# P V of a cached-attention decode kernel: from V standing to P standing in four column tiles

## Chip, cores, metric

One core of a Trainium2 chip. The metric is the time of one execution of the whole program in microseconds (us), as the device measures it; the median of three runs is compared. The profile is one further execution, taken by the hardware profiler.

## What is computed

One decode step for 8 sequences: attention over the last 2048 positions of a cache, then an MLP block. Cut to what matters here:

```
q = layernorm(x) @ wq                         # 8 x 32 heads x 128
k, v = last 2048 positions of the caches      # 8 sequences x 8 kv heads x 2048 x 128
p = softmax(q k^T / sqrt(128))                # 4 query heads share a kv head
o = p v                                       # the step that is changed
h = x + o @ wo
out = h + B(layernorm(h))                     # B: w3, gelu, w4 (its token shift is zero for S = 1)
```

k and v are 33.5 MB each in bfloat16; with wq, wo, w3 and w4 the kernel reads 79.18 MB.

## The kernel before

**Units.** The work on the caches is cut into 16 units: unit n is sequence b = n // 2 and half t = n % 2 of its kv heads (J = 4 heads). A unit of K or V is one 2 MB load onto 128 partitions, partition 32 j + r holding 64 consecutive positions of head j. `knat` and `vnat` have four buffers each. All loads stand on SP's queue in one fixed order. A load of K waits until PE has transposed the unit that was in its buffer (`e_T`), a load of V until PE has done P V on its buffer (`e_PV`). wo comes in parts (two of 1 MB at n = 5 and 9, four of 512 KB at the end), and w3 and w4 go into freed buffers of K at the end: w3 (`sem_w3`), then w4 in three groups `sem_w4a`, `sem_w4b`, `sem_w4c`.

**One iteration of the loop over n.** PE turns the four parts of a unit of K (`turn_K`, 8 transposes in 32 bits each, L296); ACT evicts the lower half of each part (L283), DVE the upper (L284). After the third part comes the first `pe_QK`, after the fourth the second (L311: 8 matmuls of 512 columns, 32 columns of q standing, in four column tiles). P V runs three units behind K (four for the last two), one block w = 0..3 at a time (`pe_PV`), where `pvs(k)` stands.

**Softmax.** After the odd unit of a sequence: maximum (`softmax_1`, L321), two small 32-bit matmuls with DVE steps between them (`softmax_2`, `softmax_3`, L325 to L339), Exp on ACT (L342). In the next even iteration DVE spreads P into a sparse `Pz` in four parts (L355, each behind one of K's evictions), PE multiplies row sums with ones (`softmax_5`, L372), DVE takes the reciprocal (L375, L381), PE transposes P (`softmax_4`, L364) and the result `pS` is evicted by the same helper as K. The row sums, the maximum's row and column, and `turn_o`'s result share one PSUM bank, `sm`; `sm_read` holds the last DVE operation that read it, and every matmul into it waits for that.

**P V, and what follows it.** Of a block, 16 chunks of V (128 positions x 128) stand one after the other while 16 columns of P move (L397); 64 matmuls of a unit add up in 16 columns of `oT_ps`. `scale` (DVE, L407) reads them out, multiplies with the reciprocal row sums and writes `oK`; the next unit's P V waits for it. `turn_o` (4 matmuls, L417) brings the heads into the order that wo wants, and a DVE copy (L422) puts them into `o2`.

**The tail.** After the loop DVE spreads the last P (four times L355 in a row), and PE does units 12 to 15 of P V, softmax of the last sequence and wo: groups 0 to 3 after the first block of unit 15, groups 4 and 5, 6 and 7 at the end, each pair with its own load (L458). Then hsum (L559), the statistics (L562, L583), w3 (L579), gelu (L597), w4 (L607), a transpose and the store.

Operations are recorded per engine in the order in which they are written in the code, each with its waits, and emitted at the end: every engine runs its list in that order. `turn_os(to)` records `turn_o` for all units below `to` that have not had it.

Of the kernel before, what the change touches and what calls it, by code (L numbers as in the profile page):

```python
# [6 lines left out]
dt = mybir.dt  # L7
ACT = mybir.ActivationFunctionType
ALU = mybir.AluOpType
AX = mybir.AxisListType  # L10
# [3 lines left out]
H = 32  # L14
DH = 128
G = 8
R = H // G
# [11 lines left out]
NU = 2  # L29
J = G // NU  # L30
U = 4
# [5 lines left out]
NV = 4  # L37
NKT = 4
LVD = 3
WO_AT = (5, 9)  # L40
WO_G = (0, 2)
WO_L = 4
QW = 12 + R + 28
SPR = 4


# [30 lines left out]
def bass_sequential_preLN__sliding_block_cached__mixer_s_mlp__decode_kernel(  # L77
# [19 lines left out]
    NUN = NB * NU  # L97
# [4 lines left out]
    with es:  # L102
        sb = lambda shape, dtype, name: es.enter_context(nc.sbuf_tensor(name, shape, dtype))
# [4 lines left out]
        vnat = sb([128, NV, UL], dt.bfloat16, "vnat")  # L108
# [6 lines left out]
        ident_f = sb([128, 128], dt.float32, "ident_f")  # L115
# [36 lines left out]
        mK = sb([128, R], dt.float32, "mK")  # L152
        rLk = sb([128, 2, H, R], dt.float32, "rLk")
        oK = sb([128, 2, J, R, R], dt.bfloat16, "oK")
        o2 = sb([128, G, R, B], dt.bfloat16, "o2")

        NH = KC * B
        tail = Pz[:, 0, :].bitcast(dt.float32)
        at = [0]
# [30 lines left out]
        def dma(eng, dst, src, sem, *waits):  # L190
            def f(e):
# [25 lines left out]
        e_sel = DV.op(lambda e: e.tensor_reduce(sel_f[:, :].rearrange("p (j h) -> p j h", j=J),  # L217
                                                ident_f[:, :].rearrange("p (j u h) -> p j h u", j=J, u=U),
                                                AX.X, ALU.add), e_idf)
        e_mE = DV.op(lambda e: e.tensor_reduce(mE[:, :], ident_f[:, :].rearrange("p (e k) -> p e k", k=R),  # L220
                                               AX.X, ALU.max))
        e_mK = DV.op(lambda e: e.tensor_reduce(mK[:, :], ident_f[:, :].rearrange("p (e k) -> p k e", k=R),
# [41 lines left out]

        def fill_q(b):
            for c in range(2):
                at = 12 + 16 * c
# [34 lines left out]
        def pe_QK(m):  # L302
            n, v = divmod(m, 2)
            b, t = divmod(n, NU)
            lo = 12 - 8 * v - 4 * t
            kT = kT_sb[:, (2 * m) % NKT:(2 * m) % NKT + 2, :].rearrange("p u (c j r k) -> p j k (u c) r", c=8, j=J, k=2)

            def f(e):
                for k in range(2):
                    for j in range(J):  # L310
                        ins = e.matmul(S_ps[b % 2][32 * j:32 * (j + 1), :].rearrange("p (c r) -> p c r", c=16),  # L311
                                       qz[:, b % 2, J * t + j, k, lo:lo + 32], kT[:, j, k],
                                       start=(t == 0 and v == 0 and k == 0), stop=(t == NU - 1 and v == 1 and k == 1),
                                       tile_position=(0, 32 * j), skip_group_check=True)
                return ins
            e_QK[m] = PE.op(f, *e_ev[2 * m], *e_ev[2 * m + 1], e_qw[b], e_qs, e_exp.get(b - 2))
# [7 lines left out]
        def softmax_2(b):  # L324
            e_mT[b] = PE.op(lambda e: e.matmul(sm[0:1, MROW], mcol[:, :], ident_f[:, :], start=True, stop=True),  # L325
                            e_max[b], sm_read[0], e_idf)
            e = DV.op(lambda e: e.tensor_reduce(Mrow[:, :].rearrange("o (j h) -> o j h", j=J),  # L327
                                                sm[0:1, MROW].rearrange("o (j u h) -> o j h u", j=J, u=U),
                                                AX.X, ALU.max), e_mT[b])
            sm_read[0] = e  # L330
            m_bc = bass.AP(tensor=Mrow[:, :].tensor, offset=0, ap=[[H, 1], [8, J], [0, U], [1, 8]])
            e_neg[b] = DV.op(lambda e: e.tensor_scalar(negrow[:, :].rearrange("o (j u h) -> o j u h", j=J, u=U), m_bc,  # L332
                                                       -1.0, None, ALU.mult), e, e_negps.get(b - 1))

        def softmax_3(b):
# [47 lines left out]
        def V(n, w):  # L383
            if n == NUN - 1:
                return sem_vl[w], 16
            return sem_v[n % NV], 16 * (n // NV + 1)

        def pe_PV(i):
            n, w = divmod(i, U)
            b, t = divmod(n, NU)  # L390
            dst = oT_ps[:, 0:16]

            def f(e):
                for c in range(16):
                    o = (8 * (w % 2) + c // 2) * 128 + 16 * (2 * (2 * (c % 2) + w // 2) + t)
                    mvg = pS[:, b % 2, o:o + 16]
                    ins = e.matmul(dst, vnat[:, n % NV, (16 * w + c) * DH:(16 * w + c + 1) * DH], mvg,  # L397
                                   start=(w == 0 and c == 0), stop=(w == U - 1 and c == 15),
                                   skip_group_check=True)
                return ins  # L400
            e_PV[i] = PE.op(f, V(n, w), *e_pS[b], e_sc.get(n - 1))

        def scale(n):
            b, t = divmod(n, NU)
            src = oT_ps[:, 0:16]
            s_bc = bass.AP(tensor=src.tensor, offset=src.offset, ap=[src.ap[0], [1, 16], [0, R]])
            e_sc[n] = DV.op(lambda e: e.tensor_tensor(oK[:, n % 2].rearrange("p g r k -> p (g r) k"), s_bc,  # L407
                                                      rLk[:, b % 2, 16 * t:16 * t + 16, :], ALU.mult),
                            e_rL[b], e_PV[U * n + U - 1], e_scale.get(n - 2))

        def turn_o(n):
            b, t = divmod(n, NU)
# [49 lines left out]
            e_wo.append(PE.op(f, e_exp[NB - 2], X, *waits))  # L462

        def emit_PV(i):
            if i % U == 1 and i > U:
                turn_os(i // U)
                if i // U == NUN - 1:
                    pe_wo((0, 1, 2, 3), e_scale[NUN - NU], (sem_wo, 16 * len(WO_AT)))
            pe_PV(i)
            if i % U == U - 1:  # L470
                scale(i // U)

        pv = [0]
        turned = [0]

        def turn_os(to):
            while turned[0] < to:
                turn_o(turned[0])
                turned[0] += 1
# [6 lines left out]
        for n in range(NUN):  # L486
# [17 lines left out]
                fill_q(b)  # L504
            turn_K(i)
            spread(0)
            turn_os(pv[0] // U)
            turn_K(i + 1)
            spread(1)
            turn_K(i + 2)  # L510
            spread(2)
            pe_QK(2 * n)
            if t == 0 and b >= 1:
                softmax_5(b - 1)
            turn_K(i + 3)
# [17 lines left out]
        softmax_5(NB - 1)  # L533
        softmax_4(NB - 1)
        emit_PVs(NBLK)
        turn_o(NUN - 1)
        for a in range(2):
            for g in (WO_L + 2 * a, WO_L + 2 * a + 1):
                load_wo(g, sem_wl[a], 1)
# [43 lines left out]
        e = PE.op(lambda e: e.matmul(st2, ones_v[:, :], vsum[:, :], start=True, stop=True), e_vs, e_sc[NUN - 1])  # L583
# [72 lines left out]
```

## Time and profile before

| | us |
|---|---|
| runs | 197.91, 197.44, 197.72; median 197.72 |
| profiled execution | 197.34 |
| its span, first to last instruction | 196.0 |
| PE busy, matmuls | 153.8 (78% of the span) |
| PE weight loads (beside the matmuls) | 125.9 (64%) |
| DVE / ACT / POOL busy | 98.2 / 85.9 / 7.0 |
| mean granted clock of TensorE | 0.872 |
| read from HBM | 79.18 MB, 404 GB/s over the span |

The largest groups of PE are K's transposes (L296, 512 matmuls, 76.1), P V (L397, 1024, 33.2) and q K (L311, 256, 20.0). PE's matmuls are pipelined and their ends are modelled, so busy time of PE is no measure of what it could do. An idle is listed with the operation that ended it; "issue" means that the engine waited for nothing that the profile shows.

### The profile page before, as it was taken

How to read it: one execution, taken by the hardware profiler on the slowest of the kernel's cores; microseconds unless marked ns; L12 is line 12 of the kernel's file. 1: busy time of each engine (PE TensorE's matmuls, PEld its weight loads, DVE VectorE, ACT ScalarE, POOL GpSimd, SP SyncE). 2: the span in 40 equal slices, each digit the busy share in tenths (PEclk: the TensorE clock that was granted, in tenths of full speed). 3: DMA queues.
4: the chain of work that ended last, by engine and by line, in shares of the span. 5: the costliest groups of instructions: out<-in, count | busy, mean ns of one | idle time of the engine just before them, and what ended most of it. 6: DMA issues, size and time to landing. Idle time of an engine off the chain costs nothing.

```text
span 196.0 us, 5301 instructions
## 1 busy us (share of the span) xinstructions
PE 153.8 (78%) x2415; PEld 125.9 (64%) x2415; DVE 98.2 (50%) x223; ACT 85.9 (44%) x100; POOL 7.0 (4%) x28
## 2 busy tenths in 40 slices
PE   0038985978989898989885789898989897888464
PEld 0037852765869577868773668586958585777453
DVE  5302444865484566548553384549455765620130
ACT  6001565764456374735471355535635482230030
POOL 4001001001000100010001000100000000000000
PEclk9999999999699999997999579969997999555555
DMA  6999999999999999999999999999999999999970
GB/s 229 461 408 431 425 431 431 421 428 425 423 420 422 431 425 428 423 425 428 419 427 421 431 428 425 428 425 428 425 428 421 423 421 428 407 405 407 406 285 24
DMA packets 7542, 79.52 MB, mean 406 GB/s; under 512 B 856, under 2 KB 864, under 8 KB 3424
## 3 DMA queue, kind: packets, MB, share of 16 engines
q1 hardware_dynamic: 7504, 79.18, 96.1%
q8 instruction: 19, 0.31, 0.6%
q14 instruction: 3, 0.02, 0.0%
q10 hardware_dynamic: 16, 0.01, 0.0%
HBM read 79.18 MB, written 0.01 MB: 404 GB/s over the span
## 4 chain that ended last, share of the span: by engine, by line
DMA 51%; PE 31%; DVE 10%; SPq 5%; issue 2%
DMA knat<-in_A_k_cache_dram 42%; PE kT_ps L296 21%; DMA knat<-in_B_w_dram 9%; SPq L192 5%; PE S_ps L311 5%; DVE kT_sb L284 5%; DVE Pz L355 2%; PE kT_ps L364 2%; DVE mcol L321 1%; PE oT_ps L397 1%; PE sm L325 1%; PE sm L336 1%; DVE Mrow L327 1%; PE S_ps L607 1%; DVE negrow L332 0%
## 5 line engine op out<-in xcount | busy, mean ns | idle before, releaser
L283 ACT ACTIVATE kT_sb<-kT_ps 128x1024 bf16<-128x1024 bf16 x64 | 63.8, 1024 | 47.2 <-PE kT_ps L296 46.5
L296 PE MATMUL kT_ps<-perm_k,knat 128*128 128x128 f32 x512 | 76.1, 306 | 3.4 <-DMA knat<-in_A_k_cache_dram 3.2
L296 PEld LDWEIGHTS kT_ps<-perm_k,knat 128*128 128x128 f32 x512 | 65.7, 159 | 9.1 <-issue 4.3
L284 DVE TENSOR_SCALAR kT_sb<-kT_ps 128x512 int32<-128x512 int32 x64 | 44.2, 690 | 35.0 <-PE kT_ps L296 34.8
L397 PEld LDWEIGHTS oT_ps<-pS,vnat 128*128 128x128 bf16 x1024 | 30.5, 98 | 6.4 <-issue 6.1
L397 PE MATMUL oT_ps<-pS,vnat 128*128 128x16 bf16 x1024 | 33.2, 171 | 1.3 <-DVE oK L407 1.3
L311 PE MATMUL S_ps<-kT_sb,qz 128*32 128x512 bf16 x256 | 20.0, 386 | 11.0 <-DVE kT_sb L284 10.6
L355 DVE TENSOR_TENSOR Pz<-P_sb,mJ 128x512 bf16<-128x512 bf16 x32 | 21.6, 684 | 0.0
L342 ACT ACTIVATE P_sb<-S_ps,negcol 128x512 bf16<-128x512 f32 x8 | 5.5, 688 | 24.9 <-DVE negcol L339 24.9
L283 ACT ACTIVATE pS<-kT_ps 128x1024 bf16<-128x1024 bf16 x8 | 8.2, 1024 | 15.8 <-PE kT_ps L364 15.8
L311 PEld LDWEIGHTS S_ps<-kT_sb,qz 128*32 128x32 bf16 x256 | 4.7, 94 | 15.8 <-ACT kT_sb L283 14.8
L284 DVE TENSOR_SCALAR pS<-kT_ps 128x512 int32<-128x512 int32 x8 | 5.5, 692 | 9.4 <-PE kT_ps L364 9.4
L364 PEld LDWEIGHTS kT_ps<-perm_p,Pz 128*128 128x128 bf16 x128 | 8.1, 105 | 3.0 <-issue 3.0
L250 PE MATMUL S_ps<-xlnT,wbig 128*128 128x8 bf16 x128 | 3.6, 168 | 7.7 <-DMA wbig<-in_A_wq_dram 7.7
L364 PE MATMUL kT_ps<-perm_p,Pz 128*128 128x128 bf16 x128 | 9.4, 231 | 0.0
L407 DVE TENSOR_TENSOR oK<-oT_ps,rLk 128x64 bf16<-128x64 f32 x16 | 3.6, 224 | 11.1 <-PE oT_ps L397 11.1
L268 POOL COPY qz<-q_sb 64x64 bf16<-64x64 bf16 x16 | 4.6, 290 | 119.7 <-PE S_ps L311 103.5
L321 DVE TENSOR_REDUCE mcol<-S_ps 128x1 f32<-128x512 f32 x8 | 5.5, 692 | 6.5 <-PE S_ps L311 6.5
L250 PEld LDWEIGHTS S_ps<-xlnT,wbig 128*128 128x128 bf16 x128 | 3.5, 104 | 7.7 <-issue 7.7
L584 ACT ACTIVATE Pz<-oT_ps,eps 128x8 f32<-128x8 f32 x1 | 0.3, 268 | 15.0 <-PE oT_ps L583 15.0
L458 PE MATMUL S_ps<-o,wbig 128*128 128x8 bf16 x128 | 4.0, 168 | 2.3 <-issue 2.0
L255 DVE TENSOR_SCALAR kT_sb<-S_ps 128x256 bf16<-128x256 f32 x1 | 0.4, 425 | 10.0 <-PE S_ps L250 10.0
(83 smaller groups left out, 73.3 us busy)
## 6 DMA issues: line engine op xcount, KB each, us to landing
knat<-in_A_k_cache_dram SPq DMA_DIRECT2D x16, 2048.0 KB, 28.9
vnat<-in_A_v_cache_dram SPq DMA_DIRECT2D x15, 2048.0 KB, 30.8
wbig<-in_A_wq_dram SPq DMA_DIRECT2D x1, 4096.0 KB, 12.2
wbig<-in_A_wo_dram SPq DMA_DIRECT2D x2, 1024.0 KB, 30.8
vnat<-in_A_v_cache_dram SPq DMA_DIRECT2D x4, 512.0 KB, 9.4
wbig<-in_A_wo_dram SPq DMA_DIRECT2D x4, 512.0 KB, 11.8
knat<-in_B_w_dram SPq DMA_DIRECT2D x4, 448.0 KB, 13.0
knat<-in_B_w_dram SPq DMA_DIRECT2D x3, 512.0 KB, 16.6
```

Of the source, the lines that this page charges most:

```text
L192: e.dma_start(dst, src).then_inc(sem, 16)
L250: ins = e.matmul(S_ps[0][:, h * B:(h + 1) * B], wq_v[:, kc, h * DH:(h + 1) * DH], xlnT[:, kc * B:(kc + 1) * B], start=(kc == 0), stop=(kc ...
L268: e_qw[b] = PO.op(lambda e, c=c, at=at: e.tensor_copy(qz[64 * c:64 * (c + 1), b % 2, :, :, at:at + R], q_sb[64 * c:64 * (c + 1), :, :, b]. ...
L283: e_lo.append(AC.op(lambda e: e.activation(dst[:, 0:1024], ps[:, 0:1024], ACT.Copy), e_Tlo[k], *free))
L284: e_hi.append(DV.op(lambda e: e.tensor_single_scalar(dst[:, 1024:2048].bitcast(dt.int32), ps[:, 1024:2048].bitcast(dt.int32), 0, ALU.bitwi ...
L296: ins = e.matmul(ps[:, c * 128:(c + 1) * 128], src[:, c * 128:(c + 1) * 128], perm_k[:, :], is_transpose=True)
L311: ins = e.matmul(S_ps[b % 2][32 * j:32 * (j + 1), :].rearrange("p (c r) -> p c r", c=16), qz[:, b % 2, J * t + j, k, lo:lo + 32], kT[:, j, k],
L321: e_max[b] = DV.op(lambda e: e.tensor_reduce(mcol[:, :], S_ps[b % 2][:, :], AX.X, ALU.max), e_QK[4 * b + 3], e_mT.get(b - 1))
L342: e_exp[b] = AC.op(lambda e: e.activation(P_sb[:, :], S_ps[s][:, :], ACT.Exp, bias=negcol[:, s:s + 1], scale=1.0, accum_out=lcol[:, s:s + 1]),
L355: e_Pz[b, part] = DV.op(lambda e: e.tensor_tensor(Pz[:, 0, J * w * part:J * w * (part + 1)].rearrange("p (x j) -> p x j", j=J), p_bc, m_bc ...
L364: ins = e.matmul(ps[:, c * 128:(c + 1) * 128], Pz[:, 0, c * 128:(c + 1) * 128], perm_p[:, :], is_transpose=True)
L397: ins = e.matmul(dst, vnat[:, n % NV, (16 * w + c) * DH:(16 * w + c + 1) * DH], mvg, start=(w == 0 and c == 0), stop=(w == U - 1 and c == 15),
```

## The change

In a block of P V, 32 columns of P now stand and two chunks of V (256 columns) move. A block is 8 matmuls; matmul c goes to column tile c % 4, whose 32 output partitions and 256 columns of `oT_ps` it adds to. Units alternate between the two halves of the bank. Of each tile's 32 x 256 result only 16 rows of each chunk are wanted. ACT evicts 128 x 256 in 32 bits into `oE` (`evict_o`), and `fold` multiplies each of its two 128 x 128 halves, standing, with 16 columns of a 0/1 matrix `selo`, which picks the wanted rows, adds the four tiles and leaves o transposed in 16 columns of `sm`. `scale`'s multiplication reads these. For this the halves that q is placed in (`QW`, `at`, `lo`) and the row sums' and maxima's order (`sel_f`, `Mrow`, `negrow`) are rearranged.

The order changes too. A unit's fold follows the first part of K in the next iteration, where `turn_o` stood; `turn_o` follows the first `pe_QK`, directly before `softmax_5`. In the tail the fold of a unit stands after the next unit's block 0 and `turn_o` after block 1. wo's groups 0 and 1 come after block 1 of unit 15, groups 2 and 3 after block 3. The next unit's P V waits for `evict_o`.

```diff
-QW = 12 + R + 28
+QW = 24 + 32
+VP = 1
+MO = 32 * VP
+NO = 256 * VP
+TO = 128 // MO
...
+        oE = sb([128, 512], dt.float32, "oE")
+        selo = sb([128, MO], dt.float32, "selo")
...
+        e_selo = DV.op(lambda e: e.tensor_reduce(selo[:, :], ident_f[:, :].rearrange("p (a x) -> p x a", a=TO),
+                                                 AX.X, ALU.add))
...
-            lo = 12 - 8 * v - 4 * t
+            lo = 24 - 16 * t - 8 * v
...
         def pe_PV(i):
             n, w = divmod(i, U)
             b, t = divmod(n, NU)
-            dst = oT_ps[:, 0:16]
 
             def f(e):
-                for c in range(16):
-                    o = (8 * (w % 2) + c // 2) * 128 + 16 * (2 * (2 * (c % 2) + w // 2) + t)
-                    mvg = pS[:, b % 2, o:o + 16]
-                    ins = e.matmul(dst, vnat[:, n % NV, (16 * w + c) * DH:(16 * w + c + 1) * DH], mvg,
-                                   start=(w == 0 and c == 0), stop=(w == U - 1 and c == 15),
-                                   skip_group_check=True)
+                for c in range(8):
+                    o = (8 * (w % 2) + c) * 128 + 16 * (4 * t + 2 * (w // 2))
+                    q = c % TO
+                    ins = e.matmul(oT_ps[MO * q:MO * (q + 1), NO * (n % 2):NO * (n % 2 + 1)], pS[:, b % 2, o:o + MO],
+                                   vnat[:, n % NV, (16 * w + 2 * c) * DH:(16 * w + 2 * c + 2) * DH],
+                                   start=(w == 0 and c < TO), stop=(w == U - 1 and c >= 8 - TO),
+                                   tile_position=(0, MO * q), skip_group_check=True)
                 return ins
-            e_PV[i] = PE.op(f, V(n, w), *e_pS[b], e_sc.get(n - 1))
+            e_PV[i] = PE.op(f, V(n, w), *e_pS[b], e_ev_o.get(n - 1))
 
-        def scale(n):
+        def evict_o(n):
+            e_ev_o[n] = AC.op(lambda e: e.activation(oE[:, NO * (n % 2):NO * (n % 2 + 1)], oT_ps[:, NO * (n % 2):NO * (n % 2 + 1)], ACT.Copy),
+                              e_PV[U * n + U - 1], e_fold.get(n - 2))
+
+        def fold(n):
             b, t = divmod(n, NU)
-            src = oT_ps[:, 0:16]
+
+            def f(e):
+                for s in range(2 * VP):
+                    o = NO * (n % 2) + 128 * s
+                    ins = e.matmul(sm[:, 32:48], oE[:, o:o + 128], selo[:, 16 * s:16 * s + 16],
+                                   start=(s == 0), stop=(s == 2 * VP - 1))
+                return ins
+            e_fold[n] = PE.op(f, e_ev_o[n], e_selo, sm_read[0])
+            src = sm[:, 32:48]
             s_bc = bass.AP(tensor=src.tensor, offset=src.offset, ap=[src.ap[0], [1, 16], [0, R]])
...
-                            e_rL[b], e_PV[U * n + U - 1], e_scale.get(n - 2))
+                            e_rL[b], e_fold[n], e_scale.get(n - 2))
+            sm_read[0] = e_sc[n]
...
         def emit_PV(i):
-            if i % U == 1 and i > U:
-                turn_os(i // U)
-                if i // U == NUN - 1:
-                    pe_wo((0, 1, 2, 3), e_scale[NUN - NU], (sem_wo, 16 * len(WO_AT)))
+            n, w = divmod(i, U)
+            if w == 1:
+                fold_os(n)
+            if w == 2:
+                turn_os(n)
+                if n == NUN - 1:
+                    pe_wo((0, 1), e_scale[NUN - NU], (sem_wo, 16 * len(WO_AT)))
             pe_PV(i)
-            if i % U == U - 1:
-                scale(i // U)
+            if w == U - 1:
+                evict_o(n)
...
             turn_K(i)
             spread(0)
-            turn_os(pv[0] // U)
+            fold_os(pv[0] // U)
             turn_K(i + 1)
...
             pe_QK(2 * n)
+            turn_os(pv[0] // U)
             if t == 0 and b >= 1:
                 softmax_5(b - 1)
...
         emit_PVs(NBLK)
-        turn_o(NUN - 1)
+        pe_wo((2, 3))
+        fold_os(NUN)
+        turn_os(NUN)
```

More of the change, by code (lines that the diff above doesn't have):

```diff
@@ L215, in bass_sequential_preLN__sliding_block_cached__mixer_s_mlp__decode_kernel @@
                                                 ALU.subtract, ALU.mult), e)
-        e_sel = DV.op(lambda e: e.tensor_reduce(sel_f[:, :].rearrange("p (j h) -> p j h", j=J),
-                                                ident_f[:, :].rearrange("p (j u h) -> p j h u", j=J, u=U),
+        e_sel = DV.op(lambda e: e.tensor_reduce(sel_f[:, :].rearrange("p (j t h) -> p j t h", j=J, t=NU),
+                                                ident_f[:, :].rearrange("p (j t u h) -> p j t h u", j=J, t=NU, u=U),
                                                 AX.X, ALU.add), e_idf)
+        e_selo = DV.op(lambda e: e.tensor_reduce(selo[:, :], ident_f[:, :].rearrange("p (a x) -> p x a", a=TO),
+                                                 AX.X, ALU.add))
         e_mE = DV.op(lambda e: e.tensor_reduce(mE[:, :], ident_f[:, :].rearrange("p (e k) -> p e k", k=R),
@@ L266, in fill_q @@
             for c in range(2):
-                at = 12 + 16 * c
+                at = 24 + R * c
                 e_qw[b] = PO.op(lambda e, c=c, at=at: e.tensor_copy(
@@ L326, in softmax_2 @@
                             e_max[b], sm_read[0], e_idf)
-            e = DV.op(lambda e: e.tensor_reduce(Mrow[:, :].rearrange("o (j h) -> o j h", j=J),
-                                                sm[0:1, MROW].rearrange("o (j u h) -> o j h u", j=J, u=U),
+            e = DV.op(lambda e: e.tensor_reduce(Mrow[:, :].rearrange("o (x h) -> o x h", h=R),
+                                                sm[0:1, MROW].rearrange("o (x u h) -> o x h u", u=U, h=R),
                                                 AX.X, ALU.max), e_mT[b])
             sm_read[0] = e
-            m_bc = bass.AP(tensor=Mrow[:, :].tensor, offset=0, ap=[[H, 1], [8, J], [0, U], [1, 8]])
-            e_neg[b] = DV.op(lambda e: e.tensor_scalar(negrow[:, :].rearrange("o (j u h) -> o j u h", j=J, u=U), m_bc,
+            m_bc = bass.AP(tensor=Mrow[:, :].tensor, offset=0, ap=[[H, 1], [R, NU * J], [0, U], [1, R]])
+            e_neg[b] = DV.op(lambda e: e.tensor_scalar(negrow[:, :].rearrange("o (x u h) -> o x u h", u=U, h=R), m_bc,
                                                        -1.0, None, ALU.mult), e, e_negps.get(b - 1))
@@ L386, in V @@
             return sem_v[n % NV], 16 * (n // NV + 1)
+        e_ev_o, e_fold = {}, {}
         def pe_PV(i):
@@ L464, in emit_PV, with fold_os @@
         def emit_PV(i):
-            if i % U == 1 and i > U:
-                turn_os(i // U)
-                if i // U == NUN - 1:
-                    pe_wo((0, 1, 2, 3), e_scale[NUN - NU], (sem_wo, 16 * len(WO_AT)))
+            n, w = divmod(i, U)
[5 more added lines that the diff above has]
+                    pe_wo((0, 1), e_scale[NUN - NU], (sem_wo, 16 * len(WO_AT)))
             pe_PV(i)
-            if i % U == U - 1:
-                scale(i // U)
+            if w == U - 1:
+                evict_o(n)
         pv = [0]
         turned = [0]
+        folded = [0]
+        def fold_os(to):
+            while folded[0] < to:
+                fold(folded[0])
+                folded[0] += 1
         def turn_os(to):
@@ L581, in pe_w3 @@
             return ins
-        e = PE.op(lambda e: e.matmul(st2, ones_v[:, :], vsum[:, :], start=True, stop=True), e_vs, e_sc[NUN - 1])
+        e = PE.op(lambda e: e.matmul(st2, ones_v[:, :], vsum[:, :], start=True, stop=True), e_vs, e_ev_o[NUN - 1])
         e2 = AC.op(lambda e: e.activation(vv[:, 0:B], st2, ACT.Sqrt, bias=eps2[:, :], scale=1.0 + EPS), e)
```

## The prediction

> **What bounds the kernel now.** I read the page, then the windows, the timeline of the last 30 us, and last the trace's own records of DMA packets and of the sixteen marks with which each load reports that it has landed. From the page:
>
> ```profile
> PEclk9999999999699999997999579969997999555555
> DMA  6999999999999999999999999999999999999970
> q1 hardware_dynamic: 7504, 79.18, 96.1%
> q8 instruction: 19, 0.31, 0.6%
> L397 PE MATMUL oT_ps<-pS,vnat 128*128 128x16 bf16 x1024 | 33.2, 171 | 1.3 <-DVE oK L407 1.3
> ```
>
> P V is a fifth of PE's busy time, but the row of DMA is full from the second slice to the last but one: in the packet records sixteen packets are in flight at every moment from 4 to 187 us. So a faster PE gains nothing in the middle. What counts is when the last loads land and what follows them. From the timeline:
>
> ```profile
> 171.13 0.62 PE L397 MATMUL oT_ps<-pS,vnat 128*128 128x16 bf16 x16
> ...
> 171.82 1.45 PE L397 MATMUL oT_ps<-pS,vnat 128*128 128x16 bf16 x48
> ...
> 178.10 1.69 PE L458 MATMUL S_ps<-o,wbig 128*128 128x8 bf16 x58 [0.27 <-issue]
> ...
> 184.35 1.39 PE L458 MATMUL S_ps<-o,wbig 128*128 128x8 bf16 x46 [1.70 <-issue]
> 185.77 0.19 DVE L559 TENSOR_REDUCE Pz<-S_ps 128x8 f32<-128x32 f32 x1 [3.83 <-PE S_ps L458]
> ...
> 188.93 1.98 PE L579 MATMUL kT_ps<-Pz,knat 128*128 128x8 bf16 x56 [0.87 <-DMA knat<-in_B_w_dram]
> ...
> 192.68 1.01 PE L607 MATMUL S_ps<-Pz,knat 128*128 128x8 bf16 x24 [0.16 <-DMA knat<-in_B_w_dram]
> ```
>
> w3 and w4 wait for DMA. The last load (w4c, 256 KB) has its sixteen marks at 188.33 to 189.09 (seven), 190.70, 191.36 to 191.93 (six), 193.13 and 193.27: the sixteen DMA engines end 5 us apart, and the slowest sets the end; from its mark to the end of the span it is 2.73 us. What makes them unequal is q8, the fetching of PE's instructions. After its first packet (at 19.07) one mark of K's second load is late, 24.04 against 22.20 to 22.76 for fifteen; each further packet makes another engine late until eight are, the ninth (104.6) hits the first of them again, and after the seventeenth and eighteenth (181.9, 187.9) two engines have three packets. These are the marks 193.13 and 193.27; six with two packets are the marks at 191.4 to 191.9. The two idles "issue" above are the same fetching: they fall after 2124 and 2252 matmuls, 256 instructions apart with the weight loads, and end 1.35 us after a q8 packet did.
>
> **The change, part by part.**
> 1. Fewer instructions. PE has 2415 matmuls and as many weight loads, 4830 for 19 packets. P V loses 512 matmuls, and 32 fold matmuls of two rows each (as L372's x16 for 8) add 64: 1967, so 3934 instructions, 15 packets. With at most two to an engine, the marks of the two-packet engines are the last: w4c 191.93 instead of 193.27, w4b 191.30 (192.63), w3 187.77 (188.88), the last part of wo 183.03 (184.38). If PE is in time, 1.34 us go: span 194.66.
> 2. A P V block is now 8 matmuls of 256 columns in four column tiles. Not in this trace; nearest row L311, 8 of 512 columns in four tiles, next instruction 0.55 us after its start. Half the streaming gives 0.33 alone and 0.75 for three, against 0.56 and 1.4 (x16, x48). At best it is the streaming alone, 0.21; if the tiles did not overlap, 0.85 and more. I take 0.33, since L311 has the same tiles. At clock 0.5: 0.53, and 0.96 for two.
> 3. Evicting 128x256 f32 on ACT, 16 times: between L283 (1024 columns, 1.02) and L342 (512, 0.69), with 0.2 for a one-column row: 0.45. PE's next unit waits for it instead of for L407; that idle is 0.41 to 0.54 now and becomes 0.6. In the loop K's transposes cover it.
> 4. The fold: four rows as in L372, whose pair holds PE 0.25 us (0.45 at clock 0.5): 0.5 (0.9). Between K's first and second transposes it pushes QK of odd n by about 0.6, and a P V tail shorter by 0.2 follows: odd iterations 8.75 to 9.25.
> 5. turn_o moves behind QK, directly before softmax_5, whose matmul waits for turn_o's copy on DVE. That copy is queued behind an eviction and a spread (0.6 each). On the clean even iteration (69.37 to 78.40) K's fourth transposes go from 73.5 to 75.0, and QK from 75.74 to 76.9; the three blocks after it give back 0.6: 9.02 becomes 9.8. A pair is 19.05, against 19.6 us that DMA takes for two units (landings at 108.99, 118.79, 128.59). PE still waits for DMA, with less reserve.
> 6. The larger memset of qz (1408 to 1792 columns, 1.27 to 1.6 us), one more reduce on DVE (0.4) and another cut of sel_f: under the wait for wq (7.7 us idle). Nothing.
> 7. In the tail scale(11) stands behind the four spreads on DVE, and PE waits for it in the middle of unit 12.
>
> What this does to the tail, counted from the end of the last maximum chain, now at 165.31 and then at 165.55 (n=14, an even iteration without P V: 9.05 by step 5, against 8.79 now, of which 3.4 us ran at clock 0.5): spreads end +3.5, scale and turn_o +3.9, two blocks, L372's pair and 16 transposes: +5.75 (clock 1) or +7.0 (0.5; now it is +5.8). Units 13 and 14: block, fold, block, turn_o, two blocks, eviction: 2.57 each (3.64), now 2.55. Last: block, fold, block, turn_o and copy, x and wo(0,1) 1.1, two blocks, wo(2,3) 1.0 over the eviction, fold to copy 1.7, wo(4..7) 2.0: 8.1 (9.6). So L559 starts at 165.55 + 5.75 + 5.14 + 8.1 = 184.5 at full clock, 165.55 + 7.0 + 7.28 + 9.6 = 189.4 at half, against 185.77. From L559 to the end, when no load is late, it is 8.7 us (table load of gelu ending +4.05, w4 from +4.3, 2.0, then 2.3). So L559 may start as late as 186.0 without costing; beyond that each us costs one.
>
> **The clock decides.** In the trace's records the granted clock changes only on a grid of 3.41 us; windows on it:
>
> ```profile
> 162.83:166.24 3.41, 2.57 (x66) 2.03 (x62) 1.65 (x6) 0.78 (x2) 0.00 (x0) 1.00 0.98 418
> 166.24:169.66 3.42, 2.51 (x70) 2.37 (x67) 2.78 (x7) 0.00 (x0) 0.00 (x0) 0.50 1.00 422
> 169.66:173.07 3.41, 3.41 (x83) 3.36 (x82) 1.48 (x4) 2.51 (x3) 0.00 (x0) 0.50 0.98 396
> 173.07:176.48 3.41, 2.52 (x85) 2.35 (x82) 0.68 (x3) 0.00 (x0) 0.00 (x0) 0.50 1.03 408
> ```
>
> Seventh column: the granted clock; it falls at 166.24 and stays at 0.5 although PE is busy 2.5 us of each 3.4. Counting columns streamed instead (16 per matmul, QK's tiles by a quarter, without L364's 16-bit transposes when cold), every window below 0.7 us at full clock was followed by 0.5, none above 0.75; from 0.5 it came back after 1.4 us and more, not after 1.2. The new blocks stream 0.21 us against 0.11, so the drops inside the loop should go. In the tail the wait for the spreads leaves two blocks in a window, 0.5: a drop near 169.7 is likely, and with 1.6 us per cold window from unit 13 on a return at 173.1 or 176.5. One cold window costs 1.25 at the 16 transposes (L559 at 185.8), a second 1.07 in unit 13 and 0.2 in the next block (187.0). I take both as my forecast: span 194.7 to 195.7, middle 195.1. The profiled run is 1.34 above its span (197.34), and the median of the runs, 197.72, is 0.38 above that: 196.8.
>
> **Rivals.**
> - PE warm throughout: L559 at 184.5, DMA alone sets the end, span 194.66, 196.4. For it: the blocks stream twice as much. Against it: the windows above. [...] Chance 0.20.
> - PE cold to the end, as now: L559 at 189.4, and the PE chain takes the place of the late DMA engines. Span 198.1, 199.8 in the runs' terms: slower. It decides once L559 starts after 187.3 (196.0 less 8.7). Chance 0.20.
> - The loop becomes PE's. If the drops at the start of even iterations stay (1 us per pair: 9.98 to 10.16 against the clean 9.02), or the tiles do not overlap, a pair takes 20.1 or more, units 10 to 15 fall 1 to 3 us behind, and the tail with them: 199 to 201. Chance 0.14.
> - The packets do not matter as I read them (the fetches fall on other engines): the end stays at 196.0, 197.7. Chance 0.13.
> - My forecast: 0.33.
>
> **How the numbers follow.** A difference under 0.2%, 0.4 us, is what a measurement can't tell from none. The forecast lies mostly below that, with an end that touches it (0.04 of its 0.33); with the warm case, faster 0.49. Same: that 0.04 and the last rival, 0.17. Slower: 0.34. The range 196.1 to 199.9 takes in the warm case, the forecast, no change, the cold case and the mild half of the loop case; its worse half (0.07), and something that none of the cases holds, stay out.
>
> **What would show it.** 15 or 16 q8 packets; w4c's last mark near 191.9; no idle "issue" of 1.7 us before wo; P V blocks of 0.33 us; L372 in even iterations 1 us later; clock 0.5 from about 169.7 and back by 176.5; L559 near 186. Wrong if the last mark stays at 193.3, if PE waits no more for K's loads after n=10, or if L559 starts after 187.3.

## The result and the profile after

| | before | after |
|---|---|---|
| median of 6 runs, us | 197.47 (197.25 to 197.91) | 199.89 (198.69 to 200.91) |
| profiled execution, us | 197.34 | 198.69 |
| its span, us | 196.0 | 197.3 |
| mean granted clock | 0.872 | 0.908 |
| q8 packets | 19 | 15 |
| last mark of the last load (w4c) | 193.27 | 192.01 |
| hsum (L559, now L594) starts | 185.77 | 188.94 |

The kernel became slower: ratio 1.0114, 95% interval 1.007 to 1.0158. Ratios and intervals, here and below, leave out runs that are more than 1.5% above the fastest of their kernel. The six runs spread over 2.2 us, against 0.66 before, and the profiled one is the fastest of them. From the page of the changed kernel, the rows that answer to those shown of before, with the chain's shares by engine:

```profile
PEclk9999999999999996999999999969999999555555
DMA  6999999999999999999999999999999999999940
q8 instruction: 15, 0.25, 0.5%
PE 47%; DMA 25%; DVE 22%; issue 2%; ACT 2%; SPq 0%; DVEq 0%
L406 PE MATMUL oT_ps<-vnat,pS 128*32 128x256 bf16 x512 | 27.4, 308 | 2.3 <-ACT oE L414 2.3
```

DMA was 51% of the chain before and is 25% now. The row of DMA shows the same in its last two digits, 4 and 0 where 7 and 0 stood: the loads are through earlier, and the kernel isn't. P V's busy time went from 33.2 to 27.4 us, and the loop has two windows at half clock where it had six; neither is where the end is decided. That is where the row PEclk ends in 555555: the tail runs at half clock, as it did before. The timeline of the changed kernel's tail (start, duration, engine, line, operation, what it writes and reads, count, idle before it and what ended that):

```profile
166.64 0.40 PE L406 MATMUL oT_ps<-vnat,pS 128*32 128x256 bf16 x8 [1.10 <-ACT oE L414]
...
169.09 0.20 PE L440 MATMUL sm<-oK,mE 128*32 128x16 bf16 x4 [1.10 <-DVE oK L429]
...
170.54 1.89 PE L372 MATMUL kT_ps<-perm_p,Pz 128*128 128x128 bf16 x16
172.36 0.62 PE L406 MATMUL oT_ps<-vnat,pS 128*32 128x256 bf16 x8
172.91 1.04 PE L423 MATMUL sm<-selo,oE 128*128 128x16 f32 x4
...
175.96 0.62 PE L406 MATMUL oT_ps<-vnat,pS 128*32 128x256 bf16 x8 [0.58 <-ACT oE L414]
...
179.55 0.62 PE L406 MATMUL oT_ps<-vnat,pS 128*32 128x256 bf16 x8 [0.58 <-ACT oE L414]
...
187.03 1.87 PE L481 MATMUL S_ps<-o,wbig 128*128 128x8 bf16 x64 [0.33 <-DVE o L445]
188.94 0.19 DVE L594 TENSOR_REDUCE Pz<-S_ps 128x8 f32<-128x32 f32 x1 [1.97 <-PE S_ps L481]
...
191.08 1.95 PE L614 MATMUL kT_ps<-Pz,knat 128*128 128x8 bf16 x56
193.31 1.65 PE L642 MATMUL S_ps<-Pz,knat 128*128 128x8 bf16 x56 [0.28 <-ACT Pz L632]
```

A unit of P V takes 3.60 us (172.36, 175.96, 179.55), more than a third of it the fold of 1.04 and the 0.58 in which PE waits for ACT's eviction. w3 (L614) waits for nothing any more, and w4 (L642) only for ACT's gelu: all their loads have come. The balance: hsum is 3.17 us later. From it to the end it is 8.34 us, so before, with hsum at 185.77, PE could have ended at 194.1, 1.9 us ahead of the DMA-bound 196.0. 3.17 less 1.9 is the 1.3 us by which the span grew.

### The profile page after: what moved, and what is told of

It is laid out like the page before. It is cut to its first block, busy times and chain, and to the rows that moved or that the text cites. A ratio compares the mean times of both kernels' runs of the same rounds, so it can differ in the third digit from the quotient of the medians.

```text
span 197.3 us, 4428 instructions
## 1 busy us (share of the span) xinstructions
PE 147.1 (75%) x1967; PEld 110.1 (56%) x1967; DVE 99.3 (50%) x224; ACT 90.6 (46%) x116; POOL 7.3 (4%) x28
## 2 busy tenths in 40 slices
DMA packets 7538, 79.46 MB, mean 403 GB/s; under 512 B 856, under 2 KB 864, under 8 KB 3424
## 3 DMA queue, kind: packets, MB, share of 16 engines
q1 hardware_dynamic: 7504, 79.18, 95.5%
HBM read 79.18 MB, written 0.01 MB: 401 GB/s over the span
## 4 chain that ended last, share of the span: by engine, by line
PE 47%; DMA 25%; DVE 22%; issue 2%; ACT 2%; SPq 0%; DVEq 0%
DMA knat<-in_A_k_cache_dram 25%; PE kT_ps L304 21%; DVE kT_sb L292 9%; PE S_ps L319 6%; DVE Pz L363 6%; PE oT_ps L406 6%; PE kT_ps L372 4%; PE sm L423 3%; DVE mcol L329 2%; PE S_ps L481 2%; PE sm L380 1%; PE sm L344 1%; PE sm L333 1%; DVE Mrow L335 1%; PE S_ps L642 1%
## 5 line engine op out<-in xcount | busy, mean ns | idle before, releaser
L304 PE MATMUL kT_ps<-perm_k,knat 128*128 128x128 f32 x512 | 68.1, 285 | 3.1 <-DMA knat<-in_A_k_cache_dram 2.9
L304 PEld LDWEIGHTS kT_ps<-perm_k,knat 128*128 128x128 f32 x512 | 59.4, 148 | 9.8 <-issue 4.7
L406 PE MATMUL oT_ps<-vnat,pS 128*32 128x256 bf16 x512 | 27.4, 308 | 2.3 <-ACT oE L414 2.3
L406 PEld LDWEIGHTS oT_ps<-vnat,pS 128*32 128x32 bf16 x512 | 11.8, 102 | 8.7 <-issue 5.7
L414 ACT ACTIVATE oE<-oT_ps 128x256 f32<-128x256 f32 x16 | 6.1, 379 | 16.3 <-PE oT_ps L406 16.3
L423 PEld LDWEIGHTS sm<-selo,oE 128*128 128x128 f32 x64 | 10.0, 224 | 2.3 <-issue 1.4
L423 PE MATMUL sm<-selo,oE 128*128 128x16 f32 x64 | 10.8, 284 | 0.0
L372 PEld LDWEIGHTS kT_ps<-perm_p,Pz 128*128 128x128 bf16 x128 | 8.8, 111 | 3.4 <-issue 3.4
L372 PE MATMUL kT_ps<-perm_p,Pz 128*128 128x128 bf16 x128 | 10.2, 243 | 0.0
L429 DVE TENSOR_TENSOR oK<-sm,rLk 128x64 bf16<-128x64 f32 x16 | 3.5, 219 | 10.6 <-PE sm L423 10.6
L380 PE MATMUL sm<-lsel,ones_f 128*128 128x32 f32 x16 | 3.5, 302 | 7.1 <-DVE o L445 7.1
## 6 DMA issues: line engine op xcount, KB each, us to landing
wbig<-in_A_wo_dram SPq DMA_DIRECT2D x4, 512.0 KB, 11.3
```

Of the source, the lines that this page charges most:

```text
L304: ins = e.matmul(ps[:, c * 128:(c + 1) * 128], src[:, c * 128:(c + 1) * 128], perm_k[:, :], is_transpose=True)
L372: ins = e.matmul(ps[:, c * 128:(c + 1) * 128], Pz[:, 0, c * 128:(c + 1) * 128], perm_p[:, :], is_transpose=True)
L380: e_Lb[b] = PE.op(lambda e: e.matmul(sm[:, LB], ones_f[:, :], lsel[:, :], start=True, stop=True), e_lsel[b], sm_read[0])
L406: ins = e.matmul(oT_ps[MO * q:MO * (q + 1), NO * (n % 2):NO * (n % 2 + 1)], pS[:, b % 2, o:o + MO], vnat[:, n % NV, (16 * w + 2 * c) * DH: ...
L414: e_ev_o[n] = AC.op(lambda e: e.activation(oE[:, NO * (n % 2):NO * (n % 2 + 1)], oT_ps[:, NO * (n % 2):NO * (n % 2 + 1)], ACT.Copy), e_PV[ ...
L423: ins = e.matmul(sm[:, 32:48], oE[:, o:o + 128], selo[:, 16 * s:16 * s + 16], start=(s == 0), stop=(s == 2 * VP - 1))
```

## Experiments

The theory after the result: the change shortens the DMA's end by fewer packets, as forecast, and loses that and more because PE's tail runs at clock 0.5. The rivals: the packets have nothing to do with it; the loop is to blame (the wait before softmax_5, iterations made late).

**P V halved in the kernel before.** Every second chunk of P V is left out.

```diff
-                for c in range(16):
+                for c in range(0, 16, 2):
```

> The kernel before with every second chunk of P V left out (its o is wrong): 512 matmuls and weight loads fewer, so as few instructions as the change has, and none of its other parts. If the fetching of PE's instructions sets when the last loads land: 15 packets of q8 instead of 19, no DMA engine with three before the end, last mark of w4c at 191.9 instead of 193.3, span 194.7, 196.1 us, 0.7% faster than before. If the marks are late for another reason: last mark 193.3, span 196.0, no difference to before.

Measured: 196.06 us (195.93 to 196.41), ratio 0.9928 [0.9916, 0.994]; 15 packets, w4c's last mark 192.25. Its clock is at 0.5 from 167 us to the end like the changed kernel's, but its tail is short: hsum starts at 184.03. So with fewer packets and a PE tail in time, the gain forecast for part 1 is there.

**The fold in 16 bits.** `oE` and `selo` become bfloat16.

```diff
-        oE = sb([128, 512], dt.float32, "oE")
-        selo = sb([128, MO], dt.float32, "selo")
+        oE = sb([128, 512], dt.bfloat16, "oE")
+        selo = sb([128, MO], dt.bfloat16, "selo")
...
-                                                 AX.X, ALU.add))
+                                                 AX.X, ALU.max))
```

> The changed kernel with oE and selo in 16 bits, so that the fold's two matmuls are one row each instead of two and its weights half as wide. Theory 1 (the tail's PE chain at clock 0.5 is what ends last, while the loads land 1.3 us earlier than before): the folds of units 12 to 14 fall from 0.95 us to about 0.1, the last from 1.0 to 0.25, together 3.3 us: L594 starts at about 185.6 instead of 188.94, the last load sets the end, span 194.7, 196.1 to 196.4 us, faster than before by 0.6%. Rival A (the loop's pace makes it slow, PE falls behind DMA): the folds in the loop are partly hidden, 1 us at most, 198.5 to 199. Rival B (the loads do not land earlier): 197.5.

Measured: 196.07 us (195.91 to 198.24, 12 runs), ratio 0.995 [0.9926, 0.9975]. The timeline of this kernel:

```profile
174.02 0.22 PE L423 MATMUL sm<-selo,oE 128*128 128x16 bf16 x2
...
185.52 0.19 DVE L594 TENSOR_REDUCE Pz<-S_ps 128x8 f32<-128x32 f32 x1 [1.97 <-PE S_ps L481]
...
190.11 0.99 PE L642 MATMUL S_ps<-Pz,knat 128*128 128x8 bf16 x32 [0.29 <-DMA knat<-in_B_w_dram]
191.27 1.01 PE L642 MATMUL S_ps<-Pz,knat 128*128 128x8 bf16 x24 [0.17 <-DMA knat<-in_B_w_dram]
```

The fold's row fell from 1.04 to 0.22 us, hsum came at 185.52 instead of 188.94, and w4 waits for DMA again. With a short fold, the same change is 0.5% faster than before instead of 1.1% slower. Not all of this is the fold itself: unit 13, at half clock as in the changed kernel, takes 2.78 us (173.47 to 176.25) instead of 3.60, but in this profile the clock came back at 176.00, and unit 14 took 2.08. Two of the twelve runs, those with the lowest mean clocks, took 198.06 and 198.24 all the same.

**The clock held up.** Sixteen matmuls of 512 columns, whose result nothing reads, fill PE's idle in the tail: four ahead of unit 12, six ahead of its turn_o, two ahead of units 13 to 15 each.

```diff
+        def keep(count):
...
+                for c in range(count):
+                    ins = e.matmul(kbank[2 * (k % 2) + c % 2][:, :], ident_b[:, :], vnat[:, (NUN - 4) % NV, 0:512],
+                                   start=True, stop=True, skip_group_check=True)
...
+            if n >= NUN - 4 and w == 0:
+                keep(4 if n == NUN - 4 else 2)
+            if n == NUN - 4 and w == 2:
+                keep(6)
```

> The changed kernel with 16 matmuls of 512 columns added in the tail, into a free PSUM bank, where PE waits anyway (4 before block 0 of unit 12, 6 before the turn_o that waits for the spreads, 2 before block 0 of units 13, 14 and 15); they change no result. Theory 1 with the clock as its cause: the granted clock stays at 1.0 until about 182, L372's 16 transposes take 1.07 instead of 1.9, a unit 2.6 instead of 3.6: L594 at 184.9 to 185.6, the end set by the loads, span 194.7, 196.1 to 196.4 us, the runs closer together than 2 us. Rival (the order in the tail, not the clock): the clock stays up and L594 still starts after 188. Rival A (loop): 198.5 or more.

Measured: 196.15 us (196.01 to 197.35), ratio 0.9944 [0.9926, 0.9962]; in the tail the clock is 1.0 until 184.1. From its timeline:

```profile
172.29 1.06 PE L372 MATMUL kT_ps<-perm_p,Pz 128*128 128x128 bf16 x16
...
187.04 0.17 PE L481 MATMUL S_ps<-o,wbig 128*128 128x8 bf16 x1 [0.64 <-issue]
```

The transposes take 1.06 instead of 1.89, a unit 2.50 instead of 3.60, the 32-bit fold 0.62 instead of 1.04: more work on PE made the kernel 3.7 us faster than the changed one. In this profile the last matmul of wo stood 0.64 us, in an idle marked "issue" like the two of the kernel before (0.27 and 1.70, ending 1.35 us after a q8 packet); that this one is a fetch too is an inference. hsum came at 187.24.

**The early scale.** fold(11) and turn_o(11) are recorded after the first and second of the four spreads of the last P, instead of behind all four.

```diff
+            if part == 0:
+                fold_os(NUN - 4)
+            if part == 1:
+                turn_os(NUN - 4)
```

> The changed kernel with the fold of unit 11 recorded after the first of the last four spreads and its turn_o after the second, so that DVE scales between the spreads and PE does not wait 1.4 us for them in the middle of unit 12. PE's four blocks of unit 12 then run in one piece and the transposes of P start when the last spread ends: 0.7 to 1.1 us earlier, L594 at 188.0, median 198.9, if the clock falls all the same. If this idle is what lets the clock fall: the clock stays at 1.0 in the tail, L594 at 185, 196.2.

Measured: 196.14 us (195.76 to 197.08), ratio 0.9928 [0.9905, 0.9951]. The wait for `oK` in unit 12 falls from 1.10 to 0.32 us, and in the profile the clock, after one window at 0.5 (170.25 to 173.66), is at 1.0 until 180.5. From the start of unit 15's K transposes (157.11 in the changed kernel, 158.9 here) to hsum (188.94, 187.33) it is 31.8 us there and 28.4 here: 3.4 us less, of which the wait itself is 0.8; the rest goes with the clock (a unit takes 2.50 us instead of 3.60). The edit did not keep the clock from falling: it fell at 170.25, after a window that streamed 0.70 us, and came back after one window at half clock.

**softmax_5 ahead of turn_o in the loop.**

```diff
             pe_QK(2 * n)
-            turn_os(pv[0] // U)
             if t == 0 and b >= 1:
                 softmax_5(b - 1)
+            turn_os(pv[0] // U)
```

> The changed kernel with softmax_5 recorded before turn_o instead of behind it, so that L372's matmul no longer waits for turn_o's copy on DVE in even iterations (9.6 to 9.8 us long where nothing else holds them). Theory 1 (tail): only n=14 counts, 0.5 to 0.8 us earlier tail, 199.2 us. Rival A (loop): every even iteration gains and the kernel gets 1.5 us faster or more, 198.4 or below.

Measured: 200.02 us (198.67 to 201.14), ratio 1.0124 [1.0092, 1.0155]: no gain. In the changed kernel softmax_5's matmul (L380) waited for the copy behind turn_o:

```profile
93.34 0.22 DVE L445 CAST o<-sm 128x16 bf16<-128x16 f32 x1
...
93.61 0.41 PE L380 MATMUL sm<-lsel,ones_f 128*128 128x32 f32 x2 [1.24 <-DVE o L445]
```

With the two exchanged, turn_o (L440) waits for softmax_5's reciprocal instead, since both use `sm`:

```profile
97.90 0.19 PE L440 MATMUL sm<-oK,mE 128*32 128x16 bf16 x4 [1.06 <-DVE rL L383]
```

The even iterations stayed at 9.87 us. The wait had only changed its name.

**Both moved apart.** softmax_5 directly behind the first `pe_QK`, turn_o behind K's fourth transposes.

```diff
             pe_QK(2 * n)
-            turn_os(pv[0] // U)
             if t == 0 and b >= 1:
                 softmax_5(b - 1)
             turn_K(i + 3)
+            turn_os(pv[0] // U)
```

> The changed kernel with softmax_5 directly behind pe_QK and turn_o behind K's fourth transposes, so that neither of the two waits of 1.1 to 1.25 us for DVE (L380's for turn_o's copy, or turn_o's for the reciprocal) stands in front of those transposes. Even iterations fall from 9.85 to 8.7 us. If PE's lateness at the end of the loop (0 in the profiled run of the change, 1.9 us in that of e4) makes the slow runs: it is gone, all runs lie within 1 us, and with n=14 0.9 us shorter the median is 197.6 to 198.0. If the lateness counts for nothing: 199.0, spread as before.

Measured: 197.84 us (nine runs, 196.28 to 199.17; three more from 199.78 to 200.45, and 198.14 is the median of all twelve), ratio 1.0022 [0.9996, 1.0048]. Even iterations take 8.80 us where the clock is full and no load is waited for, and are no longer the longer ones. The median is 2.05 us below the changed kernel's (1.75 with all twelve runs), but the runs still spread over far more than the 1 us expected. So the order of these two is worth some 2 us of the median. Through what is not shown: in the one profile (199.17 us) PE is not late, since unit 14 begins at 148.21 with its load landed at 148.17, yet the tail is cold from 165.5 to the end and hsum comes at 189.42.

**The three edits together** (16-bit fold, both moved apart, early scale).

> 16-bit fold, the order of e6 in the loop and that of e7 before the tail, together. The PE chain of the tail starts 0.9 us earlier and is 4 us shorter than the change's: the loads alone set the end in every run, last mark of w4c 191.9, span 194.6, 196.0 us, no run above 196.6.

Measured: 196.13 us (195.91 to 196.25), ratio 0.9922 [0.9904, 0.994]. This beats both kernels, in every run. From its timeline:

```profile
172.75 0.40 PE L406 MATMUL oT_ps<-vnat,pS 128*32 128x256 bf16 x8 [0.98 <-DMA vnat<-in_A_v_cache_dram]
...
187.73 1.96 PE L618 MATMUL kT_ps<-Pz,knat 128*128 128x8 bf16 x56 [1.17 <-DMA knat<-in_B_w_dram]
...
191.48 1.01 PE L646 MATMUL S_ps<-Pz,knat 128*128 128x8 bf16 x24 [0.18 <-DMA knat<-in_B_w_dram]
```

PE waits for V, for w3 and for w4; hsum starts at 184.28 and w4c's last mark is 192.06.

**Packets alone, by padding.** The 16-bit fold with 230 tiny transposes ahead of q, to bring two packets back.

```diff
+        def pe_pad(e):
+            for c in range(230):
+                ins = e.matmul(xT_ps[:, 128:128 + B], xln_b[:, 0:128], ident_b[0:B, 0:B], is_transpose=True)
+            return ins
+        PE.op(pe_pad, e_xT)
```

> The kernel with the 16-bit fold (196.07 us) and 230 idle transposes of 8 columns added on PE at the start, where it waits 7 us for wq: 460 instructions more, 17 packets of q8 instead of 15; nothing else changes and no result does. If the number of packets sets the end: the 17th falls on a DMA engine that has two, the last mark of w4c is at 193.1 to 193.3 instead of 191.86 (one or two marks), span 195.9, 197.3 us. If packets do not matter: last mark 191.9, 196.1 us.

Measured: 196.54 us (eleven runs, 195.83 to 198.49; one more at 199.29), ratio 0.9959 [0.9932, 0.9985]; 17 packets, but w4c's last mark at 192.09. This settles nothing: the 16th and 17th packets fell at 190.2 and 193.9, too late to hold up an engine whose work was nearly done, and in this profile (198.46 us) hsum came only at 188.70, so that PE and not the loads set the end.

**Packets alone, by cutting matmuls.** The three edits together, with each matmul of P V cut into two of 128 columns: the same columns, and 512 more matmuls and weight loads.

```diff
-                    ins = e.matmul(oT_ps[MO * q:MO * (q + 1), NO * (n % 2):NO * (n % 2 + 1)], pS[:, b % 2, o:o + MO],
-                                   vnat[:, n % NV, (16 * w + 2 * c) * DH:(16 * w + 2 * c + 2) * DH],
...
+                    for h in range(2):
+                        ins = e.matmul(oT_ps[MO * q:MO * (q + 1), NO * (n % 2) + h * DH:NO * (n % 2) + (h + 1) * DH], pS[:, b % 2, o:o + MO],
+                                       vnat[:, n % NV, (16 * w + 2 * c + h) * DH:(16 * w + 2 * c + h + 1) * DH],
...
```

> The version with all three edits (16-bit fold, softmax_5 and turn_o later in the loop, fold(11) and turn_o(11) earlier), with each matmul of P V cut into two of 128 moving columns: the same columns streamed and the same result, but 512 more matmuls and 512 more weight loads, so some 19 packets of the TensorE's instruction queue instead of 15. If the packets set when the last load lands: the packets come back to 18 or 19, 17 of them before 188 us, and the last mark of w4c goes from 192.06 back to 193.0-193.4; PE's tail has room (L598 was at 184.3 and may come to some 186 without moving the end), so the time is 197.1-197.5 instead of 196.13. If the packets don't matter and the DMA's end had moved for another reason (shorter P V, PE freeing buffers earlier): last mark 191.9-192.2 and 196.1-196.3. If the end is PE's after all, w4 waits for ACT's gelu and not for DMA, and the time follows L598 by 8.5-8.7 us.

Measured: 197.67 us (197.41 to 197.88, 11 runs), ratio 1.0011 [1.0002, 1.002]: the whole gain of the three edits (196.13) is gone, and no run of it comes below 197.4. The lowest runs of the five versions with 15 packets and a tail in time (P V halved, 16-bit fold, clock held up, early scale, the three edits) lie at 195.76 to 196.01. From its page and timeline:

```profile
q8 instruction: 19, 0.31, 0.7%
```

```profile
187.02 0.19 DVE L599 TENSOR_REDUCE Pz<-S_ps 128x8 f32<-128x32 f32 x1 [1.97 <-PE S_ps L482]
...
191.66 0.99 PE L647 MATMUL S_ps<-Pz,knat 128*128 128x8 bf16 x32 [0.32 <-DMA knat<-in_B_w_dram]
192.83 1.01 PE L647 MATMUL S_ps<-Pz,knat 128*128 128x8 bf16 x24 [0.17 <-DMA knat<-in_B_w_dram]
```

w4c's two last marks are 193.17 and 193.42, the other fourteen at most 191.72: two engines with three packets, as in the kernel before. w4 waits for DMA, so it is the loads that end it: hsum at 187.02 and 8.34 us behind it would have ended at 195.4, and the span is 196.2. That only two marks moved speaks against a PE that frees buffers later. In these kernels the packets set the DMA's end: 192.06 with 15 of them, 193.42 with 19.

**When the clock comes back.** Two kernels, each the changed one with matmuls of 512 columns added: two ahead of units 13, 14 and 15 each, and eight in one go ahead of unit 13.

```diff
+            if n >= NUN - 3 and w == 0:
+                keep(2)
```

> The changed kernel with two matmuls of 512 columns (whose result nothing reads) ahead of each of units 13, 14 and 15. It asks when the clock comes back. In the ten traces so far, with a column-tiled matmul counted by its share of the array, every 16-bit matmul by its columns and every 32-bit one (K's transposes, the fold) by twice its columns, 84 windows of 3.41 us at clock 0.5 that streamed 2.45 us or less were all followed by another one; of the 41 that streamed 2.49 us or more, 40 were followed by clock 1.0. The prediction had counted 32-bit operands once and so had put the bound at 1.4 us. The cold windows of units 13 and 14 streamed 1.5 to 1.7 us; the two added matmuls are 0.85 us per unit at clock 0.5, of which 0.58 fill the wait for the eviction, so the windows go to 1.9-2.3 us. By the bound of 1.4 the clock comes back by 178; by the bound of 2.5 it stays at 0.5 to the end, a unit takes 3.9 us, and L604 (hsum) comes 0.5 to 1.0 us later than in the changed kernel, at 189.5 or later.

```diff
+            if n == NUN - 3 and w == 0:
+                keep(8)
```

> The changed kernel with eight matmuls of 512 columns (result not read) in one go ahead of unit 13, right behind the 16 transposes: 1.7 and 3.4 us of dense streaming at clock 0.5, so that one window streams 2.6 us or more wherever the grid lies. By both bounds (1.4 and 2.5 us) the clock comes back, at the latest 6.8 us after the transposes begin; the units after it then take 2.5 us instead of 3.6 and hsum comes no more than 1.5 us later than in the changed kernel although 3.4 us of work were added. If neither bound holds (something other than the columns streamed decides, such as how often PE stands), the clock stays at 0.5 and hsum comes 3 us later, at 192. Together with two matmuls for each unit: no return there and a return here speaks for the bound of 2.5, a return in both for 1.4.

Measured: 199.83 and 199.54 us, one run each (before beside them: 197.60). The windows of the first, then of the second, on the grid of the clock (stretch, its length, busy time and counts of PE, weight loads, DVE, ACT and POOL, granted clock, DMA, GB/s):

```profile
170.24:173.65 3.41, 2.25 (x34) 1.71 (x31) 1.87 (x6) 0.38 (x1) 0.00 (x0) 0.50 0.98 375
173.65:177.06 3.41, 3.19 (x24) 2.14 (x23) 0.84 (x2) 1.02 (x1) 0.00 (x0) 0.50 1.01 395
177.06:180.48 3.42, 3.42 (x42) 1.39 (x41) 0.46 (x2) 0.38 (x1) 0.00 (x0) 0.50 1.02 410
180.48:183.89 3.41, 3.16 (x56) 1.74 (x57) 0.68 (x3) 0.38 (x1) 0.00 (x0) 1.00 1.03 417
```

```profile
169.33:172.74 3.41, 2.41 (x35) 1.44 (x32) 1.92 (x6) 0.38 (x1) 0.00 (x0) 0.50 0.90 360
172.74:176.16 3.42, 3.20 (x19) 2.04 (x18) 1.06 (x3) 1.02 (x1) 0.00 (x0) 0.50 1.02 402
176.16:179.57 3.41, 2.83 (x52) 1.41 (x50) 0.46 (x2) 0.38 (x1) 0.00 (x0) 1.00 1.02 407
```

Streamed time is counted from the columns. At full clock two more of the added matmuls of 512 columns made a row 0.43 us longer in the kernel with the clock held up (six 1.47, four 1.04), and in the records of the changed kernel four matmuls of a block start within 0.01 us and the other four 0.11 us behind the first, 0.20 at half clock. So the 8 x 256 columns of a block in four tiles are put at 0.21 us at full clock and 0.43 at half, an estimate from these times. In the first kernel the cold windows streamed, by the count given in the expectation, 1.76, 1.88 and 2.64 us, and the clock came back only after the last; I had expected no window above 2.3, so its hsum (190.16) is that of a late return and not of none. One of the two matmuls ahead of unit 13 is missing from the trace; with it the second window has 2.31. In the second they streamed 1.71 and 2.99 (about 3.4 with the one of the eight that the trace misses), with the return after the second; units took 2.50 us from then on, and hsum came at 189.84, 0.9 us after the changed kernel's although 3.4 us were added. Over all thirteen traces, from before to these two (these counts replace the expectation's): of 93 windows at clock 0.5 with up to 2.46 us, none was followed by clock 1.0; of five between 2.46 and 2.6, three were; of 45 with more, all. In the traces of before and after alone, 17 windows with up to 2.40 us were followed by 0.5 again and seven with 2.88 and more by 1.0. A bound of 1.4 is ruled out by these two kernels alone. That 32-bit operands have to be counted twice is the weight which makes the windows separable: counted once, windows that returned begin at 1.32 and windows that did not reach up to 2.40. These weights are a fit to the thirteen traces and no more than that.

## Why the prediction was wrong

The sign was wrong, the time (199.89) at the upper end of the range. The rival "PE cold to the end" came true nearly to its numbers: hsum at 188.94 for its 189.4, span 197.3 for its 198.1, 199.89 for its 199.8. That the last two agree so closely is luck: the span was 0.8 us shorter than that rival had it, and the median lies 1.2 us above the profiled run instead of the 0.38 it had taken over from before.

- **Part 1, packets:** right. 15, w4c's last mark 192.01 for 191.93, w4b's 191.38 for 191.30, w3's 187.64 for 187.77, wo's 183.11 for 183.03. The kernel with the cut matmuls shows that it is the packets.
- **Part 2, the P V block:** right. In the kernel with the three edits a block holds PE 0.33 us (170.15 to 170.48), as forecast; in that with both moved apart three hold it 0.77 (58.10 to 58.87; forecast 0.75).
- **Parts 3 and 4:** right to about 0.1. ACT evicts in 0.38 (0.45), the idle behind it is 0.58 (0.6), except at unit 12, where the eviction stands behind Exp on ACT and PE waits 1.10; the fold holds PE some 0.55 us at full clock and 0.97 at half (0.5, 0.9). Odd iterations are 8.82 us at full clock, at the low end of the 8.75 to 9.25 that were forecast; the sum of a pair had taken 9.25. Which wait of the iteration took up the fold was not traced.
- **Part 5:** right. Even iterations 9.81 to 9.86 us for 9.8, waiting where it said. What it left out is that a cold window in one of them makes it 11.3 (K's n = 6, 68.14 to 79.46).
- **Part 6** cost nothing that the traces show. **Part 7** was there: 1.10 us. This wait ends at 169.09 and so did not make the clock fall at 167.73; it stands in the first cold window, which streamed 1.60 us. Without the wait it would have been 2.70, an estimate from these two numbers. Whether the wait alone kept the clock down is open: with the early scale the clock came back after one cold window, but in the kernel with softmax_5 and turn_o moved apart the wait was 0.31 us and the clock stayed at 0.5.
- **The sum of the tail:** right in both of its cases. From the maximum chain (165.41) to unit 13 6.95 us (7.0 cold), a unit 3.60 (3.64), last part 9.39 (9.6), hsum to end 8.34 (8.7). With the clock held, the units were 2.50 (2.57).
- **"The clock decides" is the step that failed.** It said that the clock comes back after a window with 1.4 us and more of streaming, and so at 173.1 or 176.5, with hsum at 185.8 to 187.0. The clock stayed at 0.5 from 167.73 to the end, and hsum came at 188.94. The windows of the changed kernel:

```profile
164.31:167.73 3.42, 1.92 (x32) 1.21 (x30) 2.07 (x7) 1.05 (x3) 0.00 (x0) 1.00 1.01 426
167.73:171.14 3.41, 2.31 (x36) 1.53 (x29) 1.90 (x5) 0.38 (x1) 0.00 (x0) 0.50 0.96 399
171.14:174.55 3.41, 3.41 (x45) 2.46 (x46) 1.21 (x3) 1.02 (x1) 0.00 (x0) 0.50 1.01 404
174.55:177.97 3.42, 2.84 (x44) 1.63 (x40) 0.45 (x2) 0.38 (x1) 0.00 (x0) 0.50 1.02 402
```

The fall came 2 us earlier than expected (167.73 for 169.7), after a window with 0.69 us, in which PE had waited 1.10 us for the eviction behind Exp. Then the windows streamed 1.60, 2.40, 1.57 and 1.73 us, all above 1.4 and all below 2.46. By the prediction's own count (32-bit columns once, L372's transposes left out) they are 0.92, 1.26, 1.51 and 1.68: the 1.6 us for a cold window of units 13 and 14 was about right, but no return followed, so the bound was wrong. The bound of 1.4 had been read from windows of the loop, full of K's 32-bit transposes, which I counted once, though 16 of them take 1.94 us at full clock where 16 of L372's 16-bit ones take 1.06. Counted twice, the windows of the kernel before that were followed by a return had 2.88 us and more. Nothing in the new tail reached that: a unit streams 1.7 us in its 3.6, because a block's four column tiles stream side by side (four matmuls start within 0.01 us) and the fold (0.97 us) and the wait for the eviction (0.58) hold PE while little streams. I also left out L372's transposes when cold; the window from 170.25 in the kernel with the early scale (2.88 us with them, 1.2 without) came back, so they count.

So do K's 32-bit transposes. In the kernel with the three edits PE works in the window from 139.16 to 142.57 on 16 of K's transposes and the last 0.11 us of a fold, at 0.5, and the clock is 1.0 after it:

```profile
139.12 3.61 PE L304 MATMUL kT_ps<-perm_k,knat 128*128 128x128 f32 x16
```

- **The loop rival** (0.14) does not show in the profiled run. The loop has two windows at half clock instead of six, and with even iterations of 9.8 us a cold one makes the next unit late (unit 13 began at 139.31, its load had landed at 138.34), but before it began at 139.17. Unit 14 is on time in both (148.17, before 148.22), and the tail begins at 165.41 for 165.31: the loop cost 0.1 us here. That the order in the loop matters in the median is shown by the kernel with softmax_5 and turn_o moved apart, some 2 us below.

What stays open: whether the other runs of the changed kernel, up to 200.91, are late from the loop or from the tail. Only the fastest is profiled. Their order follows the mean clock (0.908 for the fastest, 0.883 for the slowest), and e.g. the kernel with softmax_5 ahead of turn_o, profiled at span 199.2, began unit 14 at 150.04, 2.1 us after its load had landed (147.98); that is a likeness, not a proof.

## What to carry to other kernels

Cost an added step of PE at both granted clocks, and find out which it will have in its place: a fold of 0.55 us per unit in the middle of DMA-bound work was free in the profiled run (the tail began at 165.41 for 165.31), and in the tail, at half clock, four folds of 0.97 us cost more than the change had gained (1.26 us in the last mark). In this case's traces the clock went with what PE streamed per window of 3.41 us (32-bit operands twice, column tiles by their share), not with how dense its row looks: in the changed kernel the window from 171.14, with PE busy 3.41 of 3.41 us and 2.40 streamed, was followed by half clock. Whether the same count tells the clock of another kernel was not shown. When a wait is moved between two users of one buffer, ask what the other of them then waits for.

## What the runs showed of the hardware that was not expected

- The return of the clock, counted in the thirteen traces of this case with weights fitted to them: 1.0 followed none of the 93 windows at 0.5 with up to 2.46 of 3.41 us streamed, and all 45 with more than 2.6. The fall is less sharp: every window at full clock with under 0.95 us fell (37), none with over 1.33 did, and between them 24 of 76 windows fell.
- Added matmuls that compute nothing made the changed kernel 3.7 us faster; in its tail the same rows run at full clock (a unit of P V 2.50 us instead of 3.60).
- Four packets of 16 KB of PE instructions (19 against 15), 0.06 MB beside 79.18 MB, were worth 1.26 us in the last mark (before against after) and 1.54 us in the time (the cut matmuls against the three edits). After the first packet of before one of a load's sixteen marks is late (24.04, the others at most 22.76); after eighteen, w4c's latest are 193.13 and 193.27, the other fourteen at most 191.93, and w4's last matmuls wait for DMA. In the kernel with the cut matmuls PE also stood 3.70 us in the middle of wo, in an idle marked "issue"; DMA's end covered it.
